# A new order table, its second gate ahead of a buffer's reuse, and column means of w1 in place of a centring matrix

## The chip, the cores and the metric

One core of a Trainium2 chip. The metric is the device time of one execution in microseconds (us), on one core. The kernel runs five engines, each with its own fixed order of instructions: PE (TensorE, matmuls), DVE (VectorE), ACT (ScalarE), POOL (GpSimd) and SP (SyncE), which issues most loads and stores. Executions of one kernel agree within about 1 per cent here; some are in a slower state, which is told by its time and mostly goes with a lower clock. Medians and ranges are over all runs; ratios, and what is called the mean of the fast runs, leave the slow ones out. "Ratio" is the mean time of one kernel's fast runs over that of the other's fast runs of the same rounds on the same chip, so it is not quite the ratio of the medians that are quoted. The figure in brackets is its 95% interval.

## The reference, cut to what matters

```python
# q, k, v, a_re, a_im: (4, 8, 768, 48) float32
scale = min(|a|, 0.999) / (|a| + 1e-6);  a = a * scale      # complex decay
for t in range(768):
    S = a[t] * S + k[t] (x) v[t]                            # 48 x 48 a head, complex
    y[t] = q[t] @ Re(S)
x = y as (4, 768, 384)
xn = (x - mean(x)) / sqrt(var(x) + 1e-6) * g_ln
out = x + relu(xn @ w_ch1) @ w_ch2                          # 384 -> 1536 -> 384
```

The kernel does the recurrence in chunks of 128 steps: logarithm and angle of the decay are summed by matmuls, k and q are scaled by the exponentials and by sine and cosine (`ke`, `qe`, `ks`, `qs`), transposed, and multiplied (`am`, `atm`, `y`). Two chunks are a pair, and there are 12 pairs. The subtraction of the mean and g_ln are folded into w_ch1 once, at the start. "First-layer matmuls" are those with `w1b`, "second-layer" those with `w2b`.

## The kernel before: the parts that matter

Every operation is named (`l.3.0` is l of pair 3), and one table fixes the order of all of them on all engines. The letter is the engine, the digit a PSUM bank.

```python
RINGS = {"are": 3, "aim": 3, "q": 3, "k": 3, "vf": 2, ...}        # buffers of each tile
GATES = {"gate.0": "k.0.1", "gate.1": "aim.1.0"}
PLAN = """
... aim.3.0:S tab.trig.0:A th.0.0:A decc.0:V2 ph.0.0:P3
th.0.1:A aim.4.0:S th.1.0:A ...                                   # load of aim, pair 4
...
cos.2.0:A cos.1.0:A pad.ks.1:G gate.1:G ksT.1:V7 ...              # gate.1, much later
... v.0:G pad.qs.1:G ... qe.1.0.0:G ... wl.1:G ...                # POOL's order behind it
"""
# Graph.run: a buffer is checked only through the "uses" that an operation declares
for kind, idx in op.uses:
    for n in touch.get((kind, idx - self.rings[kind]), ()):
        assert n in done, (op.name, n)

def T(name, i):
    return tiles[name][i % RINGS[name]]                           # aim of pair 4 is aim of pair 1

def gate(name, t):                                                # no uses declared
    g.add(name, lambda: nc.gpsimd.tensor_copy(out=probe, in_=t()[:, 0, 0:1]), needs=[GATES[name]])
gate("gate.0", lambda: T("k", 0)[:, 1])
gate("gate.1", lambda: T("aim", 1))
# wl.0 and wl.1: POOL issues the loads of w1b and w2b behind gate.0 and gate.1

# mean folded into w1: gc = (I - 1/384) * g_ln; for each of 3 x 3 blocks (128 rows, 512 columns)
# 3 matmuls ("wp") and one write-back ("wc"): 27 matmuls, 9 copies on DVE or ACT
nc.tensor.matmul(bank(o), lhsT=gc[:, dc, ts(ec, C)], rhs=w1b[:, dc, ts(jb, 512)], ...)

# l: two DVE instructions
nc.vector.scalar_tensor_tensor(out=l, in0=r2, scalar=0.5, in1=w, op0=ALU.mult, op1=ALU.add)
nc.vector.tensor_scalar(out=l, in0=l, scalar1=LNCAP, scalar2=LNEPS, op0=ALU.min, op1=ALU.add)
```

Of the kernel before, what the change touches and what calls it, by code (L numbers as in the profile page):

```python
# [9 lines left out]
FP32 = mybir.dt.float32  # L10
# [23 lines left out]
GATES = {"gate.0": "k.0.1", "gate.1": "aim.1.0"}  # L34
# [5 lines left out]
ue:G car0.1:G are.0.0:S pad.ks.0:G car0.0:G tab.log.0:A ln.0.0:A iv.0.0:A ident:G cmat.0:G are.0.1:S one:G  # L40
zdec:G aim.0.0:S r.0.0:V ln.0.1:A iv.0.1:A aim.0.1:S are.1.0:S are.2.0:S aim.1.0:S r.0.1:V r2.0.1:V r2.0.0:A
u.0.0:A k.0.0:S gln:S k.0.1:S q.0.1:S aim.2.0:S q.0.0:S u.0.1:A ln.1.0:A iv.1.0:A uth:V vf.0.0:S vf.0.1:S
l.0.0:V warm.0:P1 warm.1:P1 warm.2:P1 warm.3:P1 warm.4:P1 warm.5:P1 warm.6:P1 warm.7:P1 warm.8:P1 warm.9:P1
warm.10:P1 warm.11:P1 warm.12:P1 warm.13:P1 warm.14:P1 warm.15:P1 warm.16:P1 warm.17:P1 warm.18:P1
warm.19:P1 warm.20:P1 warm.21:P1 warm.22:P1 dec.0.0:P0 l.0.1:V pick:G ln.2.0:A iv.2.0:A dec.0.1:P1 en.0.1:A1
en.0.0:A0 r.1.0:V r2.1.0:V e.0.1:A1 u.1.0:A cmat.1:G k.1.1:S q.2.0:S q.1.0:S ke.0.1.0:V q.1.1:S are.3.0:S
gate.0:G are.4.0:S vf.1.1:S k.1.0:S vf.1.0:S q.2.1:S e.0.0:A0 warm.23:P3 warm.24:P3 warm.25:P3 warm.26:P3
warm.27:P3 warm.28:P3 warm.29:P3 warm.30:P3 warm.31:P3 warm.32:P3 warm.33:P3 warm.34:P3 warm.35:P3
warm.36:P3 warm.37:P3 warm.38:P3 warm.39:P3 warm.40:P3 warm.41:P3 warm.42:P3 warm.43:P3 warm.44:P3 dps.0:P2
l.1.0:V warm.45:P3 warm.46:P3 warm.47:P3 dec.1.0:P4 aim.3.0:S tab.trig.0:A th.0.0:A decc.0:V2 ph.0.0:P3  # L50
th.0.1:A aim.4.0:S th.1.0:A ph.0.1:P2 r.2.0:V r2.2.0:V ke.0.0.0:V car.0.0:A3 abs.0.0:A3 cos.0.0:A car.0.1:V2
qe.0.1.0:V warm.48:P1 warm.49:P1 warm.50:P1 ph.1.0:P6 k.2.0:S k.2.1:S sin.0.0:A3 qe.0.0.0:V q.3.1:S
qs.0.0.1:V ks.0.0.0:V sin.0.1:A2 th.2.0:A abs.0.1:A2 cos.0.1:A car.1.0:V6 ph.2.0:P0 wl.0:G pad.qs.0:G
qs.0.1.1:V qs.0.0.0:V ks.0.0.1:V qs.0.1.0:V ks.0.1.0:V ks.0.1.1:V warm.51:P2 qT.0:P3 qsT.0:V3 sin.1.0:A6
abs.1.0:A6 kT.0:P2 ksT.0:V2 qT.1:P6 kT.1:P7 abs.2.0:A0 sin.2.0:A0 am.0:P2 cmat.2:G wgc:V pad.ks.2:G mask:G
cos.2.0:A cos.1.0:A pad.ks.1:G gate.1:G ksT.1:V7 qsT.1:V6 tab.log.1:A e.1.0:A4 atm.0:V2 wp.1.1:P0 wp.1.2:P1
wp.1.0:P7 wc.1.1:V0 wp.2.2:P6 am.1:P2 v.0:G pad.qs.1:G wp.2.1:P0 wc.1.0:V7 atm.1:V2 en.1.0:A4 gm.0:P7
u.2.0:A y.0:P4 qe.1.0.0:G G.0:A7 qe.1.0.1:G wp.0.1:P5 wp.2.0:P2 wc.1.2:V1 wl.1:G y.1:P3 x.0:A4 ln.3.0:A
qs.1.0.0:V l.2.0:V wc.2.2:A6 x.1:A3 wc.2.0:A2 xtr.0:P1 wp.0.2:P4 wp.0.0:P6 qs.1.0.1:V wc.0.1:V5 wc.2.1:A0
gm.1:P7 G.1:V7 wc.0.2:A4 aim.5.0:S q.3.0:S dec.2.0:P2 wc.0.0:A6 bn.1:V xtr.1:P0 xT.1:A0 xT.0:V1 e.2.0:A2  # L60
ke.1.0.1:G ke.1.0.0:G ks.1.0.1:V ks.1.0.0:V en.2.0:A2 iv.3.0:A ln.4.0:A v.1:A qT.3:P5 qT.2:P4 dps.1:P7
vf.2.1:S vf.2.0:S qe.2.0.1:G mm1.0.1.1:P0 mm1.0.1.0:P0 kT.3:P6 pad.qs.2:G qsT.3:V5 qsT.2:V4 kT.2:P2
mm1.0.0.1:P4 mm1.0.0.0:P4 relu.0.1:V0 ksT.2:V2 bn.0:V mm1.0.2.0:P0 k.3.0:S am.2:P2 qe.2.0.0:G ksT.3:A6
relu.0.0:A4 decc.1:A7 r.3.0:G gm.2:P6 qs.2.0.0:V mm1.0.2.1:P0 am.3:P4 iv.4.0:A G.2:A6 r2.3.0:A qs.2.0.1:V
qT.5:P7 gm.3:P6 atm.2:V2 atm.3:V4 y.2:P2 mm2.1.0:P3 y.3:P4 mm2.0.0:P5 mm2.1.1:P3 relu.0.2:V0 u.3.0:A r.4.0:G
rstd.0:G l.3.0:V x.2:A2 xtr.2:P2 mm2.0.1:P5 mm2.1.2:P3 x.3:V4 mm2.0.2:P5 k.4.0:S dec.3.0:P0 xtr.3:P4 k.3.1:S
ke.2.0.1:V r2.4.0:A u.4.0:A tab.trig.1:A th.3.0:A G.3:V6 qsT.5:V7 xT.2:A2 ot.1:V3 xT.3:V4 are.6.0:S
ke.2.0.0:G ks.2.0.1:G tab.log.2:A en.3.0:A0 ph.3.0:P6 e.3.0:A0 ot.0:V5 l.4.0:V ks.2.0.0:G mm1.1.0.0:P2
mm1.1.0.1:P2 dps.3:P4 qT.4:P5 mm1.1.1.1:P0 relu.1.0:V2 mm1.1.1.0:P0 mm2.2.0:P2 qsT.4:V5 decc.3:V4
tab.trig.2:A th.4.0:A mm1.1.2.1:P4 sin.3.0:A6 kT.4:P3 mm1.1.2.0:P4 bn.3:V abs.3.0:A6 qe.3.0.0:V qe.3.0.1:V  # L70
qs.3.0.1:V relu.1.1:A0 ksT.4:V3 cos.3.0:A v.2:G ke.3.0.1:G dec.4.0:P0 car.3.0:V6 relu.1.2:A4 mm2.3.0:P3
mm2.3.1:P3 mm2.3.2:P3 am.4:P6 gm.4:P4 mm2.2.1:P2 are.5.0:S ksT.5:S aim.6.0:S bn.2:V tab.log.3:A e.4.0:A0
en.4.0:A0 am.5:P0 G.4:A4 ke.3.0.0:G ks.3.0.1:V qs.3.0.0:V atm.4:V6 qT.6:P5 ks.3.0.0:G y.4:P4 kT.6:P6 kT.7:P7
atm.5:V0 y.5:P0 mm2.2.2:P2 ke.4.0.0:G ln.5.0:A rstd.1:G iv.5.0:A r.5.0:G ln.6.0:A x.4:A4 st.0:S x.5:A0
ksT.6:V6 st.1:S vf.4.0:S qsT.6:V5 dps.4:P6 xtr.5:P1 xtr.4:P0 am.6:P4 vf.3.0:S vf.3.1:S ksT.7:V7 decc.4:V6
iv.6.0:A tab.trig.3:A th.5.0:A r.6.0:G ph.4.0:P6 abs.4.0:A6 sin.4.0:A6 r2.6.0:A q.4.0:S xT.5:V1 xT.4:V0
mm1.2.2.0:P0 mm1.2.2.1:P0 q.4.1:S qe.4.0.0:G k.4.1:S vf.4.1:S car.4.0:A6 bn.4:V atm.6:V4 ot.2:V2 ot.3:V3
mm1.2.0.1:P4 mm1.2.0.0:P4 bn.5:V mm1.2.1.0:P2 v.3:G gm.6:P6 mm1.2.1.1:P2 qe.4.0.1:G y.6:P7 v.4:G relu.2.2:V0
relu.2.0:V4 x.6:V7 G.6:A6 ph.5.0:P0 relu.2.1:A2 ke.4.0.1:G qsT.7:S am.7:P4 k.5.1:S atm.7:V4 qs.4.0.1:G
mm2.4.0:P7 gm.7:P6 mm2.5.0:P2 r2.5.0:V are.7.0:S vf.5.0:S q.5.1:S th.6.0:A mm2.4.1:P7 sin.5.0:A0 cos.4.0:A  # L80
ks.4.0.0:V qs.4.0.0:V xtr.6:P3 y.7:P4 ks.4.0.1:V mm2.5.1:P2 mm2.5.2:P2 mm2.4.2:P7 x.7:V4 xtr.7:P5 qT.8:P4
rstd.2:G G.7:V6 xT.6:V3 tab.log.4:A u.5.0:A l.5.0:V abs.5.0:A0 u.6.0:A vf.5.1:S gm.8:P6 st.2:S q.5.0:S
oa.5:A2 v.5:G ot.5:G xT.7:A5 ln.7.0:A qsT.8:V4 are.8.0:S dec.5.0:P0 ot.4:V7 en.5.0:A0 e.5.0:A0 mm1.3.0.0:P2
mm1.3.0.1:P2 mm1.3.1.1:P4 mm1.3.1.0:P4 relu.3.0:A2 l.6.0:V qe.5.0.1:V G.8:V6 k.5.0:S relu.3.1:V4 ksT.8:S
ksT.9:S dec.6.0:P0 mm1.3.2.0:P2 mm1.3.2.1:P2 ln.8.0:A gm.9:P6 am.8:P4 mm2.6.0:P7 iv.7.0:A en.6.0:A0
ke.5.0.0:G ke.5.0.1:G aim.7.0:S qe.5.0.0:G qsT.9:S st.4:S q.6.1:S q.6.0:S k.6.0:S k.7.0:S e.6.0:A0 r.7.0:G
bn.7:V relu.3.2:V2 ph.6.0:P0 am.9:P2 atm.8:V4 mm2.7.0:P4 y.8:P5 iv.8.0:A tab.trig.4:A sin.6.0:A0 th.7.0:A
mm2.6.1:P7 qs.5.0.1:V r2.7.0:G qe.6.0.0:G atm.9:V2 y.9:P2 mm2.6.2:P7 mm2.7.1:P4 aim.8.0:S st.3:S vf.6.0:S
car.6.0:A0 x.8:A5 bn.6:V rstd.3:G x.9:V2 G.9:V6 bn.9:V ks.5.0.1:V abs.6.0:A0 cos.5.0:A qs.5.0.0:V cos.6.0:A
mm2.7.2:P4 xtr.9:P5 xtr.8:P6 ph.7.0:P2 oa.7:A4 ks.5.0.0:V qe.6.0.1:G ke.6.0.0:G xT.8:A6 dps.6:P4 xT.9:V5  # L90
r.8.0:G vf.6.1:S k.6.1:S ot.6:V7 car.7.0:A2 decc.6:V4 qT.10:P0 kT.10:P1 kT.11:P6 gm.10:P7 mm1.4.0.0:P4
mm1.4.0.1:P4 qsT.10:V0 abs.7.0:A2 qsT.11:S bn.8:V sin.7.0:A2 ksT.10:A1 am.10:P2 mm1.4.1.1:P0 ksT.11:V6
are.9.0:S vf.7.0:S st.5:S q.7.0:S G.10:V7 mm1.4.1.0:P0 am.11:P6 cos.7.0:A th.8.0:A tab.log.5:A u.7.0:A
relu.4.0:V4 ke.6.0.1:G qs.6.0.1:G relu.4.1:A0 v.6:G r2.8.0:A atm.10:V2 atm.11:V6 l.7.0:V qs.6.0.0:V
ks.6.0.1:V ks.6.0.0:V are.10.0:S mm1.4.2.1:P4 mm1.4.2.0:P4 ph.8.0:P2 y.11:P6 x.11:A6 y.10:P7 x.10:A7
ln.9.0:A dec.7.0:P0 q.7.1:S e.7.0:A0 en.7.0:A0 aim.9.0:S st.6:S iv.9.0:A rstd.4:G u.8.0:A qe.7.0.0:G ot.7:G
k.7.1:S vf.7.1:S mm2.8.0:P6 mm2.9.0:P7 mm2.8.1:P6 relu.4.2:V4 xtr.10:P4 xtr.11:P5 mm2.8.2:P6 xT.11:V5
xT.10:V4 mm2.9.1:P7 mm2.9.2:P7 bn.10:V r.9.0:V r2.9.0:V oa.8:A6 abs.8.0:A2 mm1.5.0.0:P0 mm1.5.1.1:P4
mm1.5.0.1:P0 kT.12:P6 mm1.5.1.0:P4 l.8.0:V ksT.12:V6 tab.trig.5:A sin.8.0:A2 relu.5.1:V4 mm1.5.2.0:P2
gm.12:P6 mm1.5.2.1:P2 k.8.0:S qsT.12:S qsT.13:S q.8.1:S am.12:P4 th.9.0:A ot.9:V7 relu.5.0:A0 ke.7.0.1:G  # L100
G.12:A6 qe.7.0.1:G qs.7.0.0:V qs.7.0.1:V ksT.13:S ph.9.0:P0 atm.12:V4 relu.5.2:A2 ke.7.0.0:G ks.7.0.1:V
ks.7.0.0:G gm.13:P6 am.13:P2 mm2.11.0:P7 vf.8.1:S q.8.0:S mm2.10.0:P4 mm2.10.1:P4 qT.14:P5 cos.8.0:A
sin.9.0:A0 car.9.0:V0 vf.8.0:S are.11.0:S k.8.1:S abs.9.0:A0 atm.13:V2 cos.9.0:A v.8:G y.12:P0 dec.8.0:P2
v.7:G y.13:P1 mm2.10.2:P4 G.13:V6 qsT.14:V5 bn.11:V k.9.0:S st.7:S gm.14:P6 dps.7:P5 tab.log.6:A en.8.0:A2
e.8.0:A2 u.9.0:A rstd.5:G ot.8:G aim.10.0:S x.12:V0 x.13:V1 xtr.13:P0 xtr.12:P1 ksT.14:S ksT.15:S qsT.15:S
# [93 lines left out]
def kernel(  # L199
# [12 lines left out]
    nc = tc.nc  # L212
# [559 lines left out]
```

## Time and profile before

| | before |
|---|---|
| time, median of 4 (range) | 209.06 us (207.92 to 211.78) |
| span of the profiled run | 206.8 us |
| first first-layer matmul | 46.67 us |
| last second-layer matmul ends | 203.31 us |
| PE, DVE, ACT, POOL busy | 176.3, 168.0, 156.9, 106.7 us |

In the groups by line and shape, a row gives line, engine, operation, tile written and read, count, then busy us, mean ns of one, and the idle time in front:

```profile
L455 DVE SCALAR_TENSOR_TENSOR l<-r,w 128x768 f16<-128x768 f16 x11 | 13.7, 1241 | 1.0 <-ACT r L451 1.0
L457 DVE TENSOR_SCALAR l<-l 128x768 f16<-128x768 f16 x11 | 7.7, 704 | 0.4
```

These are l's two steps: 1241 and 704 ns in the mean, while undisturbed ones take 951 and 360. The rest I read as time in which DVE stands behind POOL at the port they share.

### The profile page before, as it was taken

The numbers are of one execution on the slowest core, as the hardware profiler recorded it, in microseconds if no ns is written. First come the engines' busy times: TensorE is split into PE (matmuls) and PEld (weight loads), VectorE is DVE, ScalarE is ACT, GpSimd is POOL, SyncE is SP. The second block draws the span as 40 slices with busy tenths as digits, with TensorE's granted clock in tenths as the row PEclk, the third lists the DMA queues.
The fourth block names the chain that finished last, engine by engine and source line by source line (L and its number), as shares of the span: only waits on it lengthen the run. The fifth ranks groups of instructions, "written<-read, shape, count | busy, mean of one in ns | idle before, by whom it ended". The sixth has DMA issues, their size and how long they took to land.

```text
span 206.8 us, 5060 instructions
## 1 busy us (share of the span) xinstructions
PE 176.3 (85%) x1999; PEld 132.6 (64%) x2001; DVE 168.0 (81%) x276; ACT 156.9 (76%) x219; POOL 106.7 (52%) x131
## 2 busy tenths in 40 slices
PE   5666930689998899989979997997999899999993
PEld 4444710367766588677658674786687677977771
DVE  0679960299999899999999899799998997774752
ACT  5799960389999999999979894898799958743210
POOL 8472000858756579649794491355457813514330
PEclk9999995599999999999999997899999999999998
DMA  5999999999808995979989999999999989695322
GB/s 141 281 223 205 176 267 250 225 163 193 207 4 118 257 199 122 240 128 249 217 157 259 230 178 190 241 174 230 176 225 230 174 100 235 170 203 109 116 76 76
DMA packets 135271, 38.34 MB, mean 185 GB/s; under 512 B 130256, under 2 KB 134864, under 8 KB 135248
## 3 DMA queue, kind: packets, MB, share of 16 engines
q1 hardware_dynamic: 133296, 35.66, 83.6%
q0 software_dynamic: 1952, 2.36, 6.8%
q8 instruction: 15, 0.25, 0.5%
q14 instruction: 8, 0.07, 0.2%
HBM read 28.31 MB, written 4.72 MB: 160 GB/s over the span
## 4 chain that ended last, share of the span: by engine, by line
PE 42%; DVE 31%; issue 18%; POOL 7%; ACT 1%; POOLq 0%; DVEq 0%
PE banks L706 14%; PE banks L685 13%; DVE l L455 5%; DVE atm L277 4%; PE banks L590 4%; DVE ks L277 3%; DVE h L698 3%; PE banks L483 2%; DVE qs L277 2%; DVE stats L653 2%; PE banks L465 2%; PE banks L640 2%; DVE x L274 1%; PE banks L567 1%; DVE ot L720 1%
## 5 line engine op out<-in xcount | busy, mean ns | idle before, releaser
L706 PE MATMUL banks<-w2b,h 128*128 128x384 bf16 x288 | 54.1, 327 | 2.6 <-DVE G L277 1.2
L685 PE MATMUL banks<-xT,w1b 128*128 128x256 bf16 x432 | 52.5, 272 | 0.1
L685 PEld LDWEIGHTS <-w1b 128*128 128x128 bf16 x432 | 41.1, 98 | 6.5 <-DVE xT L274 0.3
L706 PEld LDWEIGHTS <-h 128*128 128x128 bf16 x288 | 26.5, 98 | 17.1 <-issue 2.8
L277 DVE TENSOR_TENSOR atm<-banks,mask 128x1024 bf16<-128x1024 f32 x24 | 28.9, 1215 | 4.7 <-PE banks L590 4.2
L696 ACT ACTIVATE h<-banks 128x1024 bf16<-128x1024 f32 x20 | 20.4, 1022 | 11.1 <-PE banks L685 11.0
L277 DVE TENSOR_TENSOR qs<-qe,trig 128x768 bf16<-128x768 bf16 (+1 forms) x23 | 13.5, 606 | 11.4 <-POOL qe L277 11.1
L277 POOL TENSOR_TENSOR qe<-q,e 128x384 bf16<-128x384 f32 x16 | 17.4, 1090 | 8.8 <-ACT e L469 5.9
L698 DVE TENSOR_SCALAR h<-banks 128x1024 bf16<-128x1024 f32 x16 | 19.3, 1212 | 2.8 <-PE banks L685 2.8
L740 ACT ACT_TABLE_LOAD x16 | 20.5, 1283 | 1.1 <-PEq L756 0.8
L277 POOL TENSOR_TENSOR ke<-k,en 128x384 bf16<-128x384 f32 x16 | 16.5, 1042 | 5.6 <-ACT en L469 2.9
L277 POOL TENSOR_TENSOR r<-aim,are 128x768 f16<-128x768 f32 x8 | 14.9, 1859 | 8.2 <-ACT are L439 7.6
L618 PE MATMUL banks<-v,ks 128*128 128x48 bf16 x160 | 7.5, 186 | 12.2 <-POOL v L403 10.4
L618 PEld LDWEIGHTS <-ks 128*128 128x128 bf16 x160 | 7.0, 99 | 14.4 <-issue 10.8
L455 DVE SCALAR_TENSOR_TENSOR l<-r,w 128x768 f16<-128x768 f16 (+1 forms) x13 | 14.7, 1135 | 1.0 <-ACT r L451 1.0
L590 PE MATMUL banks<-qsT,ksT 128*128 128x128 bf16 x192 | 15.0, 223 | 0.3 <-DVE h L698 0.2
L272 ACT CAST G<-banks 128x384 bf16<-128x384 f32 x9 | 4.3, 478 | 14.0 <-PE banks L618 13.9
L403 POOL TENSOR_SCALAR v<-vf 128x768 bf16<-128x768 f32 x11 | 10.3, 942 | 8.0 <-PE banks L483 4.6
L277 DVE TENSOR_TENSOR ks<-ke,trig 128x768 bf16<-128x768 bf16 (+1 forms) x21 | 13.8, 680 | 0.2
L590 PEld LDWEIGHTS <-ksT 128*128 128x128 bf16 x192 | 12.4, 99 | 1.9 <-issue 0.5
L718 POOL TENSOR_TENSOR ot<-ot,x 128x384 f32<-128x384 f32 x9 | 8.3, 931 | 9.7 <-ACT ot L711 9.7
L653 DVE BATCH_NORM_STATS2 stats<-x 128x6 f32<-128x384 bf16 x24 | 13.1, 548 | 0.1
(90 smaller groups left out, 395.8 us busy)
## 6 DMA issues: line engine op xcount, KB each, us to landing
k<-in_k_dram SPq DMA_DIRECT2D x24, 192.0 KB, 4.4
q<-in_q_dram SPq DMA_DIRECT2D x24, 192.0 KB, 3.7
vf<-in_v_dram SPq DMA_DIRECT2D x24, 192.0 KB, 4.1
out_dram<-ot SPq DMA_DIRECT2D x24, 192.0 KB, 2.8
are<-in_a_re_dram SPq DMA_DIRECT2D x11, 384.0 KB, 4.6
aim<-in_a_im_dram SPq DMA_DIRECT2D x11, 384.0 KB, 4.7
w1b<-in_moe_w_ch_dram POOLq DMA_DIRECT2D x1, 1152.0 KB, 10.5
w2b<-in_moe_w_ch_dram POOLq DMA_DIRECT2D x1, 1152.0 KB, 12.5
```

The source lines that it names most:

```text
L277: {"DVE": nc.vector, "POOL": nc.gpsimd}[eng(name)].tensor_tensor(**kw)
L403: {"DVE": nc.vector, "POOL": nc.gpsimd}[eng(nm)].tensor_scalar(out=T("v", P), in0=T("vf", P), scalar1=1.0, scalar2=0.0, op0=ALU.mult, op1= ...
L455: nc.vector.scalar_tensor_tensor(out=S_("l"), in0=S_("r2"), scalar=0.5, in1=S_("w"), op0=ALU.mult, op1=ALU.add)
L590: nc.tensor.matmul(ps[:, h], lhsT=T("ksT", n)[:, h], rhs=T("qsT", n)[:, h], start=True, stop=True)
L618: nc.tensor.matmul(heads(ps)[:, h], lhsT=T("ks", P)[:, c, h], rhs=T("v", P)[:, c, h], start=nfirst, stop=True, skip_group_check=True)
L653: nc.vector.bn_stats(out=T("stats", n), in_=T("x", n))
L685: nc.tensor.matmul(ps[:, jj], lhsT=w1b[:, dc, ts(gi * JG + jj, C)], rhs=T("xT", P)[:, dc].rearrange("p c t -> p (c t)"), start=(dc == 0), ...
L696: act(out=dst, in_=src, func=AF.Relu)
L698: nc.vector.tensor_scalar(out=dst, in0=src, scalar1=0.0, scalar2=None, op0=ALU.max)
L706: nc.tensor.matmul(bank(f"o.{n}")[:, 0:DM], lhsT=T("h", P)[:, j, ts(c, C)], rhs=w2b[:, j], start=(j == 0), stop=(j == NJ - 1))
L718: nc.gpsimd.tensor_tensor(out=T("ot", n), in0=T("ot", n), in1=T("x", n), op=ALU.add)
L740: g.add(f"tab.{nm}.{i}", lambda tab=tab: nc.scalar.preload_act_table_set(tab))
```

## The change

Its intent: a new order table found by a search that models the shared port ("taken in turns"), so that DVE and POOL should hinder each other less; a gate that declares which buffer it reads; and fewer matmuls for the folded mean, since g_ln * (w - column mean) needs only the column means. The transposition xT may also go by DMA, and does so for 2 of 24. The table also moves work between engines (relu from DVE to ACT, ks from DVE to POOL). It is 100 lines, and is cut here.

```diff
-GATES = {"gate.0": "k.0.1", "gate.1": "aim.1.0"}
+GATES = (("k", 0, 1), ("aim", 1, 0))
 PLAN = """
-... aim.4.0:S ... wl.0:G ... gate.1:G ... v.0:G ... qe.1.0.0:G ... wl.1:G ...
+... r2.0.0:G gate.1:G q.0.0:S ... gate.0:G ... wl.0:G ... wl.1:G ... aim.4.0:S ...
-    def gate(name, t):
-        g.add(name, lambda: nc.gpsimd.tensor_copy(out=probe, in_=t()[:, 0, 0:1]), needs=[GATES[name]])
+    for i, (nm, P, c) in enumerate(GATES):
+        g.add(f"gate.{i}", lambda nm=nm, P=P, c=c: nc.gpsimd.tensor_copy(
+            out=probe, in_=(T(nm, P)[:, c] if nm in "kq" else T(nm, P))[:, 0, 0:1]),
+            needs=[f"{nm}.{P}.{c}"], uses=[(nm, P)])
-    for dc in range(ND):
-        g.add(f"cmat.{dc}", lambda dc=dc: c_cmat(dc))
+    g.add("cmean", lambda: nc.gpsimd.memset(cmean, 1.0 / DM))
     for jb in range(NG):
+        o = f"wp.{jb}"
+        def wp(jb=jb, o=o):
+            for dc in range(ND):
+                nc.tensor.matmul(bank(o), lhsT=gc[:, dc], rhs=w1b[:, dc, ts(jb, 512)],
+                                 start=(dc == 0), stop=(dc == ND - 1))
         ...
         for ec in range(ND):
-            (a wp of three matmuls, and a copy to w1b on DVE or ACT)
+            g.add(f"wc.{jb}.{ec}", lambda jb=jb, ec=ec, o=o: nc.vector.scalar_tensor_tensor(
+                out=w1b[:, ec, ts(jb, 512)], in0=w1b[:, ec, ts(jb, 512)], scalar=gln[:, ds(ec, 1)],
+                in1=bank(o), op0=ALU.mult, op1=ALU.subtract), needs=[o], ps=(o, 1))
 ...
+            (xT.n: by DMA where the table gives it to SP)
```

## The prediction

> **What bounds the kernel now.** I began with the busy table and the 40 slices, because the program runs in fixed order on five engines and the first question is whether one engine is full or all of them wait.
>
> ```profile
> PE 176.3 (85%) x1999; PEld 132.6 (64%) x2001; DVE 168.0 (81%) x276; ACT 156.9 (76%) x219; POOL 106.7 (52%) x131
> ...
> PE   5666930689998899989979997997999899999993
> ...
> DVE  0679960299999899999999899799998997774752
> ACT  5799960389999999999979894898799958743210
> POOL 8472000858756579649794491355457813514330
> PEclk9999995599999999999999997899999999999998
> DMA  5999999999808995979989999999999989695322
> ```
>
> A slice is 206.8 / 40 = 5.17 us. Three engines are near 80%, so the table names no single bound; the slices do better. In slice 6 (31.0 to 36.2 us) PE, DVE, ACT and POOL all show 0, and the PE clock is halved in slices 6 and 7. From slice 8 DVE and PE are close to full, ACT a little less. So there are three regimes: a start, a hole, and a dense part.
>
> The list of waits says what the hole is, and the order of time says when:
>
> ```profile
> POOL probe L351 <- DMA aim<-in_a_im_dram: 20.1, 1, 20.1
> ...
> DVE qs L277 <- POOL qe L277: 11.1, 1, 11.1
> ...
> PE banks L618 <- POOL v L403: 10.4, 1, 10.4
> ```
>
> ```profile
> 28.45 0.68 DVE L274 CAST w1b<-banks 128x512 bf16<-128x512 f32 x1
> ...
> 36.89 0.70 SPq L434 DMA_DIRECT2D aim<-in_a_im_dram  x1
> 37.01 0.18 POOL L351 COPY probe<-aim 128x1 f32<-128x1 f32 x1 [20.11 <-DMA aim<-in_a_im_dram]
> 37.16 0.83 POOL L403 TENSOR_SCALAR v<-vf 128x768 bf16<-128x768 f32 x1
> ...
> 38.04 0.48 PE L618 MATMUL banks<-v,ks 128*128 128x48 bf16 x8 [10.38 <-POOL v L403]
> ```
>
> One POOL instruction of 183 ns, the gate that holds back the load of the second weight, waits 20.1 us. Behind it in POOL's order stand v of pair 0 and qe of pair 1; PE waits 10.4 us for the one and DVE 11.1 us for the other. Between 29.13 (DVE's last end) and 37.01 no engine computes: 7.9 us.
>
> Why so long? The gate is meant to read aim of pair 1, the seventh load. aim has three buffers, pair 4 uses pair 1's, and in the order table before, aim.4.0 stands ahead of gate.1. The gate declares no use of the buffer, so nothing objected, and it waits for pair 4's load, the 27th of the sync queue: issued about 32, landed 37.0. The compiled order agrees: the gate waits on lane 2 of eight, and 27 is lane 2 counting from 0, while the seventh would be lane 6.
>
> Then what limits the dense part? The first-layer matmuls start at 46.67, so it lasts 160 us. The chain of waits is on DVE until about 67, mixed until 147, and from there on PE; it gives PE's true pace, which the busy time does not:
>
> ```profile
> 199.40 3.91 PE banks L706 x24
> ...
> 195.47 3.93 PE banks L685 x36
> ```
>
> That is 0.163 us for a second-layer matmul and 0.109 for a first-layer one. With 288 and 432 of these, 192 of the score products at 0.45/8, 512 small ones of 48 columns at about 0.026, and some 30 us of transposes, phases, decays and the rest, PE needs about 140 us of the 160. There are some 15 to 20 us of bubbles to win at most, plus the ends.
>
> **What the Trainium skill says.**
> 1. "SBUF — State Buffer", Who interferes with whom: a DVE instruction with two SBUF inputs contends with a GpSimd one that reads SBUF, and a DVE instruction in a 2-port mode with any GpSimd one; the later one blocks for the whole instruction. The trace agrees that DVE instructions are stretched: the large l takes 951 ns in the median of the tile view (all shapes) against a mean of 1241, its second step 360 against 704, ks 548 against 757, with single ones up to 2157.
> 2. "TensorE: Matmul & The Clock Gate", What's actually happening: an idle window of about 3.4 us halves the array's clock. The trace agrees: clock 0.50 from 32 to 40 us, and six 512-column matmuls took 2.73 us right after the hole, five 1.24 us later.
> 3. "ScalarE: Activation LUTs", What ACT_TABLE_LOAD costs: 1283 ns plus a drain of about 1380. The trace has 16 loads at a mean of 1283, but the next activation starts 0.01 us after one (13.87 + 1.28, then 15.16), so I count 1.28 only.
>
> **The change part by part.**
>
> *Gate.* It now declares its use of the buffer, and in the new table stands before aim.4.0; the compiled order shows it waiting on lane 6, the seventh load. The 7.9 us hole goes, with about 1 us of ramp (v, then qe on POOL before DVE restarts at 40.24) and about 1 us of half-clock matmuls. Against that, while nobody computed the loads ran ahead at about 260 GB/s; that lead is lost.
>
> *The new start, walked by hand along ACT,* which stands idle only about 3.6 us in the first 28. From 3.44 (the first load landed), ACT's instructions up to the second xT of pair 0, with durations from the groups by shape, sum to 6.5 (logs, exponentials, first decays) + 6.2 (table, angles, sines) + 4.9 + 4.7 + 10.2 = 32.5, of which four tables are 5.1. That is 35.9 us, about 37.5 with small waits. The first weight load is issued later than before: after ks of pair 0 and the mask on POOL, I get about 19.5 instead of 11.9; with the 10.5 us it took to land, 30, just before its first use. First layer one can thus start near 38 to 39 instead of 46.7. About **8 us** come from here.
>
> *Column means.* Instead of subtracting the mean through 27 matmuls with a centring matrix, 3 groups of 3 give the column means. 18 fewer, at 0.22 to 0.25 us in pace, is 4 us of PE, but most of it lay at 23.7 to 27.5 in the shadow of the hole and 38.7 to 43.5 after it; I count it inside the 8. The write-back was 4 on DVE at 676 and 5 on ACT at 592 ns (5.7 us); now it is 9 on DVE. The similar ot instruction of 384 columns takes 608 ns, so 512 may take about 740: 6.7 us on DVE, 4.0 more, at a place where DVE is not yet full. ACT loses 3.0. POOL loses the centring matrix, 3 x (0.42 + 0.79) = 3.6.
>
> *Moves in the dense part,* counts from the two tables times the row means. DVE: relu 16 to 9 (-8.5), ks 21 to 15 (-4.5), r2, qs, ke, r, x, car and decc (about -7), abs +5 (about +4.5), ot +5 (+3.0), v +3 (+2), ksT and xT (+1.7), write-back +4: about -5. ACT: relu +7 (+7.2), tables 16 to 20 (+5.1), abs -5 (-4.0), oa -5 (-2.9), write-back -3, rest +5: about +7, to some 164. POOL: ks +6 (+11), qs +2, r and r2 +1 each, v and ot -5 each (-9.4), centring -3.6: about +5. PE: 31 more warm-up matmuls that fill idle time, 3 more transposes.
>
> *Port in turns.* Means less medians over the large DVE instructions (l 0.29 x 11 + 0.34 x 11, ks 0.21 x 17, qs 0.11 x 19, ke 0.23 x 8, qe 0.09 x 8, r2 0.24 x 5) make about 16 us of the 168. A table whose search knew of these waits should lose fewer, and above all should not hand PE a late operand because of one. I put this at 4 us of the end, an estimate: a third of the stretch, or a quarter of PE's 15 to 20 us of bubbles.
>
> Sum: 209.6 - 8 - 4 - 1 (last stores, pieces) = **196.5 us**.
>
> **The rivals.**
> 1. *The start only.* The dense part is bound by PE at 140 us plus dependences, and ACT gets 7 us more with four more tables. Then only the 8 us remain: 201 to 202. For it: the tail from 147 is all PE. Against it: PE has visible bubbles at 104 to 108, 124 to 128 and 140 to 144 (2.5 to 2.8 us busy of 4).
> 2. *The lost lead returns as load waits.* DMA is busy in nearly every slice to 175 us[...]. For it: a shorter kernel moves the same 38.3 MB. Against it: after the start, waits on loads are some 6 us in all, and busy shares over 1.0 show that this column counts overlaps. Cost 3 to 6 us: 200 to 203.
> 3. *POOL becomes the late one.* It takes 6 more ks at 1.8 us each, against 0.55 to 0.76 on DVE. If PE or the transposes wait on them, 2 to 5 us are lost: 199 to 202.
> 4. *The search pays in full.* The stretch on DVE halves and PE runs almost without bubbles: 38.5 + 140 + 8 of bubbles + 4 for the end: 190 to 191.
>
> **Range and chances.** The hole's cause is certain and its removal worth about 4%, so within 2% (over 205.4) needs two rivals together or a new accident in the order. Range 190.5 to 203, faster 0.94, within 2% 0.05, slower 0.01.
>
> **What would show it.** Right: the gate on aim waits no more than a few us, no slice with all engines at 0, no half clock near 35, first-layer matmuls from about 38, DVE busy about 155 to 163, ACT about 164, means of l, its second step and ks nearer 951, 360 and 548. Wrong: a new wait over 5 us on POOL's ks or on a load; first-layer matmuls after 43; a dense part still 160 us long, which would make the search worth nothing; or one of 150 or less, which would make it worth more than I say.

## The result, and the profile after

| | before | after |
|---|---|---|
| time, median of 4 (range) | 209.06 (207.92 to 211.78) | 198.25 (197.11 to 198.66) |
| ratio | | 0.9491 [0.9423, 0.956] |
| span of the profiled run | 206.8 | 196.2 |
| first first-layer matmul | 46.67 | 39.68 |
| last second-layer matmul ends | 203.31 | 192.55 |

Correct, and 10.8 us faster by the medians. The page's busy row and slices (one is now 196.2 / 40 = 4.9 us):

```profile
PE 178.8 (91%) x2031; PEld 135.7 (69%) x2032; DVE 160.1 (82%) x268; ACT 164.1 (84%) x226; POOL 107.8 (55%) x127
...
PE   4987566999999999999999997999999999998992
...
DVE  1449999899999999999998799799969969935702
ACT  4799994989899999999999999897979998565160
POOL 8535558515839359135968699315891376530230
PEclk9999965599999999999999999999999999999999
DMA  5999999999899399899799999999998999994222
```

No slice has all engines at 0 any more, and PE is at 9 nearly everywhere from slice 7 on. But the PE clock still falls in slices 5 to 7. POOL's instructions in order of time (start, duration, engine, line, what, and in brackets the wait and what ended it) show the gates at work:

```profile
9.07 0.18 POOL L347 COPY probe<-aim 128x1 f32<-128x1 f32 x1 [0.63 <-DMA aim<-in_a_im_dram]
...
17.80 1.01 POOL L350 DMA_DIRECT2D w1b<-in_moe_w_ch_dram  x1
```

The gate on aim waits 0.63 us instead of 20.11. The end of the chain is the same two groups at the same pace as before:

```profile
184.71 3.93 PE banks L684 x36
188.64 3.91 PE banks L705 x24
```

So the 10.8 us come from two places: 7.0 us before the first first-layer matmul (46.67 to 39.68), and 3.8 us between it and the end (156.6 to 152.9 us). The sums of busy time from 40 us on, of before and then of after, show the second:

```profile
sum 168.00, PE 154.44 PEld 117.49 DVE 147.34 ACT 130.02 POOL 92.29; mean PE 7.35 PEld 5.59 DVE 7.02 ACT 6.19 POOL 4.39
```

```profile
sum 168.00, PE 148.94 PEld 114.82 DVE 130.94 ACT 131.98 POOL 83.93; mean PE 7.09 PEld 5.47 DVE 6.24 ACT 6.28 POOL 4.00
```

From 40 us to its last end PE is idle 163.3 - 154.4 = 8.9 us before and 152.6 - 148.9 = 3.6 us after.

The port, in the groups by shape of after:

```profile
L449 DVE SCALAR_TENSOR_TENSOR l<-r,w 128x768 f16<-128x768 f16 x11 | 11.5, 1044 | 0.3 <-ACT r L445 0.3
L451 DVE TENSOR_SCALAR l<-l 128x768 f16<-128x768 f16 x11 | 10.6, 968 | 0.4
L371 DVE SCALAR_TENSOR_TENSOR w1b<-w1b,gln,banks 128x512 bf16<-128x512 bf16 x9 | 6.1, 736 | 0.9 <-PE banks L367 0.9
```

l's first step came down (1241 to 1044 ns), its second went up (704 to 968). Instruction by instruction the reason can be seen, first DVE, then POOL:

```profile
21.98 1.86 DVE L451 TENSOR_SCALAR l<-l 128x768 f16<-128x768 f16 x1
...
31.25 1.85 DVE L451 TENSOR_SCALAR l<-l 128x768 f16<-128x768 f16 x1
```

```profile
21.78 1.84 POOL L280 TENSOR_TENSOR r<-aim,are 128x768 f16<-128x768 f32 x1 [2.98 <-ACT are L433]
...
30.36 2.52 POOL L280 TENSOR_TENSOR r<-aim,are 128x768 f16<-128x768 f32 x1 [0.50 <-ACT are L433]
```

POOL's r ends at 23.62 and 32.88, and DVE's step, 0.36 us of work, ends 0.22 us later both times (23.84, 33.10). Where no POOL instruction runs (68.36, 102.09, 130.08 us) it takes 0.36. In the second case POOL's own r, 1.81 us otherwise, took 2.52: DVE's first step was there ahead of it. Each waits for the whole instruction of the other.

### The profile page after: what moved, and what is told of

It is laid out like the page before. It is cut to its first block, busy times and chain, and to the rows that moved or that the text cites. A ratio compares the mean times of both kernels' runs of the same rounds, so it can differ in the third digit from the quotient of the medians.

```text
span 196.2 us, 5114 instructions
## 1 busy us (share of the span) xinstructions
PE 178.8 (91%) x2031; PEld 135.7 (69%) x2032; DVE 160.1 (82%) x268; ACT 164.1 (84%) x226; POOL 107.8 (55%) x127
## 4 chain that ended last, share of the span: by engine, by line
PE 50%; DVE 20%; ACT 10%; DMA 8%; SPq 5%; issue 4%; POOL 2%; DVEq 0%; POOLq 0%
PE banks L705 16%; PE banks L684 15%; DVE atm L280 5%; DMA are<-in_a_re_dram 4%; SPq L566 3%; PE banks L584 3%; DVE l L449 3%; PE banks L459 3%; DVE h L697 2%; DVE l L451 2%; PE banks L561 2%; DMA q<-in_q_dram 2%; DMA out_dram<-ot 2%; ACT L739 2%; PE banks L655 2%
## 5 line engine op out<-in xcount | busy, mean ns | idle before, releaser
L695 ACT ACTIVATE h<-banks 128x1024 bf16<-128x1024 f32 x27 | 27.0, 1022 | 5.2 <-PE banks L684 5.0
L739 ACT ACT_TABLE_LOAD x20 | 25.7, 1283 | 1.1 <-PEq L755 0.8
L280 POOL TENSOR_TENSOR ks<-ke,trig 128x768 bf16<-128x768 bf16 (+1 forms) x11 | 17.9, 1634 | 12.0 <-DVE ke L280 7.4
L280 POOL TENSOR_TENSOR r<-aim,are 128x768 f16<-128x768 f32 (+1 forms) x9 | 16.5, 1836 | 11.0 <-ACT are L433 11.0
L719 DVE SCALAR_TENSOR_TENSOR ot<-banks,rstd,x 128x384 f32<-128x384 f32 x20 | 12.0, 610 | 8.7 <-PE banks L705 6.0
L584 PE MATMUL banks<-qsT,ksT 128*128 128x128 bf16 x192 | 15.3, 227 | 1.2 <-DVE qsT L277 1.2
L734 PE MATMUL banks<-u_e 128*128 128x256 f16 x83 | 12.5, 318 | 2.8 <-POOL u_e L312 2.8
L634 PE MATMUL banks<-v,atm 128*128 128x48 bf16 x192 | 12.2, 186 | 1.5 <-DVE atm L280 1.4
L449 DVE SCALAR_TENSOR_TENSOR l<-r,w 128x768 f16<-128x768 f16 (+1 forms) x13 | 12.9, 990 | 0.9 <-ACT r L445 0.8
L634 PEld LDWEIGHTS <-atm 128*128 128x128 bf16 x192 | 10.8, 97 | 3.7 <-DVE atm L280 2.8
L734 PEld LDWEIGHTS <-u_e 128*128 128x128 f16 x83 | 9.4, 113 | 5.0 <-POOL u_e L312 2.4
L477 PE MATMUL banks<-th,u_th 128*128 128x384 f16 (+1 forms) x52 | 12.1, 320 | 0.7 <-ACT th L467 0.7
## 6 DMA issues: line engine op xcount, KB each, us to landing
w1b<-in_moe_w_ch_dram POOLq DMA_DIRECT2D x1, 1152.0 KB, 10.1
```

The source lines that it names most:

```text
L280: {"DVE": nc.vector, "POOL": nc.gpsimd}[eng(name)].tensor_tensor(**kw)
L449: nc.vector.scalar_tensor_tensor(out=S_("l"), in0=S_("r2"), scalar=0.5, in1=S_("w"), op0=ALU.mult, op1=ALU.add)
L477: nc.tensor.matmul(heads(ps[:, c]), lhsT=u_th[:, c, j], rhs=step(T("th", P), j), start=False, stop=(j == R - 1))
L584: nc.tensor.matmul(ps[:, h], lhsT=T("ksT", n)[:, h], rhs=T("qsT", n)[:, h], start=True, stop=True)
L634: nc.tensor.matmul(ps[:, h], lhsT=T("atm", n)[:, h], rhs=T("v", P)[:, c, h], start=True, stop=nfirst)
L695: act(out=dst, in_=src, func=AF.Relu)
```

## The experiments

All twelve (e1 to e3 with the changed kernel again; e7 to e10; e11, e12, e5 and e6). Each is compared with runs of the kernel before on the same chip (medians 209.49 to 210.63 us). All results are correct unless said otherwise. They fall in four questions.

| run | what it is | median us | ratio to before |
|---|---|---|---|
| after_again | the changed kernel again | 198.15 | 0.9446 [0.9384, 0.9508] |
| e1_gate | before + gate moved | 208.31 | 0.9929 [0.9857, 1.0001] |
| e2_gate_means | e1 + column means | 205.43 | 0.9749 [0.9658, 0.9841] |
| e3_means_27 | after with 27 mean matmuls | 197.42 | 0.9423 [0.9366, 0.948] |
| e7_before_smallw | before, little weight loaded | 204.17 | 0.9773 [0.9667, 0.9879] |
| e8_gate_smallw | e1, little weight loaded | 198.13 | 0.9428 [0.9345, 0.9512] |
| e9_after_smallw | after, little weight loaded | 199.83 | 0.9534 [0.9472, 0.9597] |
| e10_gate_w2late | e1, w2 load later | 208.08 | 0.9902 [0.9799, 1.0005] |
| e11_gate_pair4_late | e1, pair 4's loads later | 207.28 | 0.9882 [0.9785, 0.9979] |
| e12_after_w1_early | after, w1 load earlier | 198.7 | 0.9477 [0.9418, 0.9537] |
| e5_l_early | after, l ahead of POOL's r | 199.27 | 0.9521 [0.9443, 0.9599] |
| e6_both | e5 + PE kept busy | 200.52 | 0.9546 [0.9465, 0.9627] |

### What is the gate worth by itself?

**The gate alone.** The table of before, with one word moved:

```diff
-... th.0.1:A aim.4.0:S th.1.0:A ... pad.ks.1:G gate.1:G ksT.1:V7 ...
+... th.0.1:A gate.1:G aim.4.0:S th.1.0:A ... pad.ks.1:G ksT.1:V7 ...
```

> The kernel before with one entry of its order table moved: the gate on aim of pair 1 now stands ahead of the load of pair 4 that reuses the buffer. My theory: the stretch of 7.9 us in which no engine computes is gone with its ramp, the first-layer matmuls start near 38 to 39 us instead of 46.7, the span ends 7 to 9 us sooner (time near 200.5 to 202, ratio to before 0.96), and the half clock near 35 us is gone. Rival (the lead that the loads won in the hole was needed): the first-layer matmuls start early but waits on loads come back, and the time falls by 4 us or less (205 or more).

A miss: 208.31 us, 0.7 per cent, not clear of noise. The hole did go: the first first-layer matmul starts at 36.0 us, 10.7 us ahead of before. But l of pairs 2, 3, 4 and 5 starts at 30.9, 51.5, 58.4 and 88.7 us against 41.5, 56.1, 61.2 and 88.7: the lead is 10.6, then 4.6, 2.8 and 0. From 72 us on PE and DVE follow before's profile at nearly the same clock times. The waits (engine, line, tile, what was waited for, us in total, times, longest):

```profile
POOL qe L274 <- DMA q<-in_q_dram: 8.5, 2, 8.3
```

and POOL, in order of time:

```profile
41.64 0.92 POOL L274 TENSOR_TENSOR qe<-q,e 128x384 bf16<-128x384 f32 x1 [8.33 <-DMA q<-in_q_dram]
...
43.85 3.88 POOL L274 TENSOR_TENSOR r<-aim,are 128x768 f16<-128x768 f32 x2
```

One wait on a load has taken the place of another. q of pair 2 was issued at about 31 us and landed at 41.6; w2 (issued at 29.5) and the aim of pairs 3 and 4 (issued from 31.0 on) were under way beside it. The chain of this run goes through the aim of pair 4 (issued at 33.6, landed at 44.3), so q was not the only late load. Then POOL's backlog held the port for 3.9 us, a qs on DVE took 4.2 us, and PE stood still for 6.0 us (its clock from 40 to 72 us was 0.84 in the mean, against 0.97 before). The GB/s row of the page shows why, for before, for this run and for after:

```profile
GB/s 141 281 223 205 176 267 250 225 163 193 207 4 118 257 199 122 240 128 249 217 157 259 230 178 190 241 174 230 176 225 230 174 100 235 170 203 109 116 76 76
```

```profile
GB/s 145 273 219 199 179 265 175 211 217 250 196 144 188 178 134 62 241 163 224 231 109 267 214 164 210 253 184 250 218 153 236 156 115 205 192 214 105 116 76 76
```

```profile
GB/s 138 250 220 233 170 233 173 184 242 217 187 250 222 70 172 245 226 230 238 148 226 205 223 163 280 188 212 253 184 222 155 156 203 147 238 197 130 104 84 82
```

Summed from the left with the length of a slice, before has moved 7.98, 9.98 and 12.05 MB by 36.2, 46.5 and 56.9 us; the gate alone 7.53, 9.75 and 12.06 MB by 36.2, 46.6 and 57.0. The transfers arrive at the same clock times with or without the hole. At its first first-layer matmul, before had some 10 MB in hand and this run 7.5. The hole was the time in which the loads ran ahead. The kernel after rides nearly the same curve (7.85 MB by 39.2, 10.1 by 49.0, 12.25 by 58.9 us).

**With little weight to load.** If the loads are what takes the lead back, taking bytes away must give it back. Both weight loads are cut to a twelfth, and the rest of both weights is filled with a constant; the result is wrong.

```diff
-    out=w1b, in_=moe_w_ch1.rearrange("(dc p) j -> p dc j", p=C)), needs=["gate.0"])
+    out=w1b[:, 0, 0:DM], in_=moe_w_ch1.rearrange("(dc p) j -> p dc j", p=C)[:, 0, 0:DM]), needs=["gate.0"])
-    out=w2b, in_=moe_w_ch2.rearrange("(jc p) e -> p jc e", p=C)), needs=["gate.1"])
+    out=w2b[:, 0], in_=moe_w_ch2.rearrange("(jc p) e -> p jc e", p=C)[:, 0]), needs=["gate.1"])
+    nc.vector.memset(w1b.rearrange("p d j -> p (d j)").bitcast(FP32), 0.00996)
+    nc.vector.memset(w2b.rearrange("p d j -> p (d j)").bitcast(FP32), 0.00996)
```

On the kernel before:

> The kernel before with the two weight loads cut to one part in twelve (the rest of the weights is filled with a constant in the first 5 us on DVE), so the result is wrong on purpose; everything else, the late gate too, is as it was. It takes 2.2 of the 8.8 MB out of the first 40 us. If the loads bound the start of the program, the gate's load (the 27th) lands some us earlier and the hole shrinks: first-layer matmuls 2 to 5 us before 46.7, time 204 to 208. If the gate alone is the cause and loads are not, the time stays at 208 to 210.

Measured 204.17 us; the gate, still in its old place, waits 15.3 us instead of 20.1. On the gate alone:

> The kernel with the gate alone moved, and the same two weight loads cut (wrong result on purpose). New theory, after the gate alone gave only 0.7%: its lead of 10 us is eaten because the second weight load now leaves at 29.5 us and shares the DMA engines with the loads of pair 2 and the angles, POOL waits 8.3 us for q, and its two r that follow back to back hold DVE's qs for 4.2 us. With the weight loads gone the wait for q is under 2 us and the time falls to 199 to 202. Rival (the dense part of the old order is bound by something else and would absorb any lead): 206 or more.

Measured 198.13 us (its profiled run, slow, shows no wait of an engine on a load over 0.5 us between 26 and 80 us). So with light loads the gate is worth 0.9428 / 0.9773 = 0.965, or 6.1 us between the means of the fast runs (203.8 and 197.7); with the full loads about 1.5. **The same edit is worth 6 to 7 us or 1.5 us by whether the loads behind it arrive.** On the kernel after:

> The changed kernel with the weight loads cut in the same way (wrong result on purpose). If the new table's gain is that it fits the work to the arrival of the loads, it has little to win from lighter loads: 195 to 198. If its start is as load bound as the old one's, 190 to 193.

199.83 us, outside both ranges: no gain. The two fills stand at the head of DVE's order, and l of pair 1 starts at 22.8 us instead of 21.0, so a gain of up to 1.8 us could be hidden; the 5 us and more of a start that hangs on the weight loads could not.

### Can the old order be mended by moving a load?

**w2 later**, behind POOL's qe of pair 2:

```diff
 PLAN (of e1): wl.1:G moved from behind qe.1.0.1:G to just ahead of r.3.0:G
```

> The kernel with the gate alone moved, right result, and the second weight load moved on POOL from before ke of pair 1 to after qe of pair 2, so that q of pair 2 lands first. New theory: the wait of 8.3 us for q falls to 4 us or less, and the time lies between the gate alone (208.3) and the gate with small weights, at 202 to 206. If the order of the loads is not what ate the lead, it stays at 207 to 209.

208.08 us, a miss. The wait for q is gone, and PE waits for w2 instead:

```profile
PE banks L703 <- DMA w2b<-in_moe_w_ch_dram: 6.4, 1, 6.4
```

**Pair 4 later.**

```diff
 PLAN (of e1): are.4.0:S aim.4.0:S moved to just ahead of q.3.1:S
```

> The kernel before with gate.1 ahead of aim.4.0 as in the first experiment, and the two loads of pair 4's half (are.4.0 and aim.4.0) moved behind k.2 in the sync queue, just before q.3.1. Theory 'the old load order cannot follow the earlier start': pair 2's k and q land about 3 us sooner than in the first experiment (there q.2.1 landed at 41.6 and POOL waited 8.3 us for it), POOL's two r of pairs 3 and 4 no longer stand back to back, DVE's qs is not held for 4.2 us, and the time comes to 203 to 206. Rival 'a load moved is a wait moved': another load, r.4's or w2's, is waited for instead, and the time stays at 207 to 209.

207.28 us: the theory misses, the rival holds. The wait for q is gone, and ACT waits for what was moved:

```profile
ACT w L434 <- DMA are<-in_a_re_dram: 9.4, 2, 8.1
```

Two loads moved, and each became the wait. These two moves do not mend the old order; that no move could is not shown.

**w1 earlier in the new order**, where before had it:

```diff
 PLAN (of after): wl.0:G moved to directly behind gate.0:G (issued at 13.3 us instead of 17.8)
```

> The changed kernel with the load of the first weight issued right behind gate.0, at about 12.8 us instead of 17.8, as the old table has it. Theory 'the new table is fitted to when loads arrive': 4.7 MB of weight then goes ahead of pair 1's inputs, k, q or vf of pair 0 or 1 are waited for 2 to 6 us, first-layer matmuls start at 40 to 43 instead of 39.6 and the time is 199.5 to 202. Rival 'the start has slack for loads': same within 0.5 per cent (197.5 to 199), or the first-layer matmuls come sooner.

198.7 us, first first-layer matmul at 39.5: the rival holds. v of pair 0 came later (PE waits 2.6 us for it, and POOL's r 8.0 us on ACT's v), but the end did not move. The new order has room for this load where the old one had none for the two that were moved. (The expectation's 4.7 MB is both weights; the page puts w1 at 1152 KB as written.)

### What are the column means worth?

**Column means in the old order**, with the gate moved: one wp for each block, nine write-backs on DVE, `cmean` in place of the three `cmat`.

```diff
 (definitions of cmean, gc, wgc, wp, wc as in the change, in the kernel of e1)
-cmat.0:G ... cmat.1:G ... cmat.2:G ... wp.1.1:P0 wp.1.2:P1 wp.1.0:P7 wc.1.1:V0 ... wc.2.2:A6 ...
+cmean:G ... wp.1:P0 wc.1.1:V0 wp.2:P6 ... wc.1.0:V0 ... wp.0:P5 ... wc.2.2:V6 ...
```

> The same with the column means of the change added, in the old order: 9 matmuls of 512 columns instead of 27, the write-back 9 times on DVE at about 0.74 us instead of 4 on DVE and 5 on ACT. My theory: within 1.5 us of the run with the gate alone, because the 18 matmuls saved are 4 us at full clock in a stretch where DVE and ACT are as full as PE, and DVE gets 4 us more. Rival (the means carry much of the gain): 3 us or more faster than the gate alone. What then still lies between this and the changed kernel is the new order table: I expect 2 to 4 us.

205.43 us, from 202.59 to 205.47 in the four fast runs; two runs were slow. By the means of the fast runs (204.4 and 208.3) this is 3.9 us better than the gate alone, and the intervals of the two ratios do not overlap: my theory (within 1.5 us) misses, and the size is the rival's. In the profiled run, the fastest of the six, POOL's two r are apart (43.2 and 47.0 us), and the long qs of e1 does not occur; how much of the 2 per cent is that, and how much the means, this run cannot tell.

**All 27 matmuls in the new order.** Each accumulation is done three times, with the same result:

```diff
+            for rep in range(3):
-            for dc in range(ND):
+                for dc in range(ND):
```

> The changed kernel with each accumulation of the column means done three times over in its bank (27 matmuls as before, same result). In its profile the PE clock is half from 25 to 38 us, and the 9 matmuls take 0.43 us each in pace. If they stand on the path there, 18 more cost up to 7.7 us; the second and third group follow the decay of pair 2 directly, so I expect the first-layer matmuls 3 to 6 us later (43 to 45.5) and the time 2 to 5 us longer. If the means do not matter, as I had counted, the time is within 1 us.

197.42 us against 198.15 for the changed kernel, intervals overlapping, and the first first-layer matmul at 40.3 us instead of 39.7: 18 more matmuls cost nothing. The row of these matmuls, after and then here:

```profile
L367 PE MATMUL banks<-w1b,gc 128*128 128x512 bf16 x8 | 4.2, 630 | 0.2 <-issue 0.2
```

```profile
L368 PE MATMUL banks<-w1b,gc 128*128 128x512 bf16 x27 | 8.0, 456 | 0.0
```

PE's clock came back sooner with them (0.76 instead of 0.50 from 32 to 36 us), so that one took 456 ns instead of 630. The run asks about PE's matmuls alone, not about the write-backs or about what POOL and ACT are spared. The changed kernel itself, again, for these comparisons:

> The changed kernel unaltered, on the same chip as the partial kernels: 198 us, ratio to before 0.943 to 0.956. It is here so that the parts can be compared in one set of rounds.

### Are the port's turns and the half clock what is left?

**l ahead of POOL's r.**

```diff
 PLAN (of after): u.1.0:A l.1.0:V moved ahead of ks.0.0.0:V;  l.2.0:V moved ahead of atm.0:V2
```

> The changed kernel with l.1.0 (and u.1.0) ahead of ks.0.0.0 and l.2.0 ahead of atm.0 in the table, so that l's second step of pairs 1 and 2 starts before POOL's r does. Theory 'whoever comes second to the port waits for the whole instruction': the second step of pairs 1 and 2 takes 0.36 us instead of 1.86, first-layer matmuls start 1 to 2 us sooner (38 to 38.8), and the time is 196 to 197.7. Rival 'the end is set elsewhere, or another DVE instruction pays instead': the two steps are short but ks, r2 or another takes what they give back, and the time stays within 0.4 per cent of 198.

The rival holds, in its second form. l's second step:

```profile
L447 DVE TENSOR_SCALAR l<-l 128x768 f16<-128x768 f16 x11 | 7.7, 696 | 0.4
```

696 ns instead of 968: both 1.86 us turns are gone from l, 3.0 us in all. But they were not removed. The half-width ks and qs that now follow l stand behind POOL's r in its place, after and then here:

```profile
L280 DVE TENSOR_TENSOR ks<-ke,trig 128x384 bf16<-128x384 bf16 x3 | 1.0, 356 | 0.3 <-ACT trig L502 0.3
L280 DVE TENSOR_TENSOR qs<-qe,trig 128x384 bf16<-128x384 bf16 x4 | 2.0, 510 | 0.1
```

```profile
L276 DVE TENSOR_TENSOR ks<-ke,trig 128x384 bf16<-128x384 bf16 x3 | 2.6, 892 | 0.3 <-ACT trig L498 0.3
L276 DVE TENSOR_TENSOR qs<-qe,trig 128x384 bf16<-128x384 bf16 x4 | 3.2, 824 | 0.1
```

They take 2.8 us more. So this run does not tell what a turn is worth. e12 comes nearer to that: there both second steps take 0.36 us as well (the row is the same, 696 ns), ks and qs are not longer than after (352 and 484 ns), and the time is 198.7 us; but it moved a load too. In e5 the first first-layer matmul starts at 38.8 us, 0.9 earlier. But l of pair 3 starts at 45.7 (45.8 after), the first-layer matmuls of pair 1 at 56.0 (56.1), and the time is 199.27 us, not better than 198.15.

**The same, with PE kept busy** by 46 more warm-up matmuls between 19 and 33 us:

> As the run before (l early), with 46 more warm-up matmuls in PE's gaps between 19 and 33 us. Theory 'PE's clock is halved there because PE is idle too much': the clock stays at 0.9 or more from 25 to 38 us, the matmuls of the weight's means take 0.3 to 0.4 us instead of 0.63, and 0 to 1.5 us are won beyond the run before (195.5 to 197.5). Rival 'PE is not on the path there': clock full, time the same within 0.3 per cent. The tripled means have shown the second already for matmuls that bring the clock back; this asks it for the whole stretch.

```profile
PEclk9999999999999999999999999999999999999999
```

The clock is full throughout, and the time is 200.52 us: no gain (means of the fast runs 200.2, and 199.0 for the run before). But this does not show that the half clock is free. In the profile of the run before, the clock was 0.57 from 24 to 28 us and full from 28 on, and its mean matmuls took 378 ns already, as they do here. The 46 matmuls also stand in the way: the first first-layer matmul comes at 39.7 us instead of 38.8. And of the fast runs of e5, the three with a mean clock of 0.98 or more took 198.0 to 198.5 us, the two with 0.966 took 200.1 and 200.2. Whether the half clock costs 0 or some 2 us stays open.

## Why the prediction was right, and where a step failed

The total (196.5 predicted, 198.25 measured) lies in the range, and its two main terms, the start and the dense part, were measured nearly as written. But the trace's division by time is not the same as a division by cause, and that is where a step fails; and each of the two terms was reached by a working that is partly wrong.

- **The hole's cause: right.** The gate waited for the load of a later pair in the same buffer; it waits 0.63 us now.
- **The new start along ACT: right in time, 1 us short, only in part right in the path.** The second xT was put at 35.9 to 37.5 and ended at 38.49; the first first-layer matmul at 38 to 39, and it came at 39.68. The term "8 us" measured 7.0. There is some luck in it: ACT worked 29.9 us from 3.44 to 38.49 (32.5 predicted) and stood idle for 5.2 (1.6 allowed). Between 28 and 40 us it was busy for 8.2 of 12; the chain runs there over DVE (both long second steps of l) and PE at half clock.
- **"Its removal worth about 4%", said of the hole: wrong as a cause.** Removing the hole alone gives 1.5 us in the old order (e1), because the load lead is lost with it. That is rival 2, which I priced at 3 to 6 us for the changed kernel (against it I said that waits on loads were some 6 us in all after the start; from 40 us on they add up to 9.5 in the trace). There it doesn't hold (the longest wait on q is 3.6 us, and taking the weights' bytes away gains nothing seen); for the gate alone it holds in full, at some 9 of 10.7 us. The whole change is worth 10.8 us; the gate alone 1.5. The rest needs an order that can use the time.
- **PE's need, "about 140 us of the 160": mis-summed.** The five terms in the prediction (46.9 + 47.1 + 10.8 + 13.3 + 30) add up to 148, and the 160 us run to the end of the span; from the first first-layer matmul to the last second-layer one it was 156.6. So there were some 8 us of bubbles to win, not 15 to 20. The trace agrees with the right sum: PE was busy 148.5 us of that stretch before, and 149.3 of 152.9 after.
- **The order, "4 us": right as the dense part's gain (3.8 us; PE's idle time from 40 us on 8.9 to 3.6), by luck: it was taken as a quarter of 15 to 20 us, and is about half of 8. It is far too small as what the table does.** From the gate alone to the whole change is 0.9929 to 0.9446, some 10 us, and from the gate with column means 0.9749 to 0.9446, some 6 us. What the table owes to its order and what to the work that it moves is not separated.
- **The port's turns as its means: not shown, and the sign of one was wrong.** I expected l's second step nearer 360 ns; it rose from 704 to 968. l's first step, ks (757 to 673) and ke (778 to 547) did come down, and with the counts of after the stretch over the large instructions fell from about 16.4 to 10.4 us. What that is worth no run shows: e5 only moved the two longest turns that remain.
- **Column means: right to count them inside the 8.** The write-backs took 736 ns each (740 estimated), and PE's 18 matmuls are worth nothing there (e3). In the old order the whole of it gave about 3.9 us (e2), for a reason that is not known.
- **Engine sums: right.** DVE 160.1 (155 to 163 said), ACT 164.1 (164). POOL rose by 1.1 us, not 5.
- **No half clock near 35: wrong.** The clock was 0.69, 0.50, 0.50 and 0.60 in the four stretches of 4 us from 24 to 40 us; at full clock the time was no better (e6), but its cost is not settled.
- **Rivals 1 and 3** did not occur: the dense part did get shorter; no wait on POOL's ks over 5 us arose. **Rival 4** came true in its bubbles (3.6 us, under the 8 that it allows) and failed in its 140 us for PE, which are 149.

What stays open: which property of the new table gives its room. It consumes nearly the same bytes at the same clock times, and is at l of pair 5 at 76.0 us instead of 88.7; that it asks for loads in the order in which they arrive is what e1, e10, e11, e8 and e12 suggest together, but no run changed that alone. The new table with the gate in the old place was not run either. A further rival stands untested: the table relieves DVE (168.0 to 160.1 us busy), which held the chain until 67 us before, and no run moved that work alone. No version beat the changed kernel beyond the spread.

## What to carry to other kernels

A hole in which all engines wait is also a time in which the loads run ahead: before counting it as gain, sum the bytes moved up to its end, and ask whether the work behind it would still find its inputs. If a removed wait gives nothing, follow the lead from stage to stage (here 10.7, 4.6, 2.8, 0 us) to the wait that took it back, and test it by taking bytes away rather than by moving a load, since a moved load can become the wait itself. And a helper that reads a tile only to hold something back must declare that use: this one waited 20 us for a buffer's next owner, and no check saw it.

## What the Trainium skill lacked or had wrong

- "SBUF — State Buffer", Who interferes with whom: its rule that the port is an exclusive lock agrees with every case looked at. For a DVE instruction behind POOL's it has no figure for the end of the wait (it has one only for POOL's DMA issue behind DVE): DVE's step of 0.36 us ended 0.22 us after POOL's instruction each time (1.86 and 1.85 us in all), and POOL is held likewise (2.52 us instead of 1.81).
- "TensorE: Matmul & The Clock Gate", What's actually happening: it ties the half clock to an idle window of about 3.4 us. In the changed kernel the clock was 1.00 to 25.5 us and 0.52 in the half us after that, although PE was recorded busy for 1.69 us of the 3.5 ahead, with no gap over 1.31 us. (In e5, with 0.28 us busy from 20 to 24, the clock was 0.57 from 24 to 28, as the page has it.) A later section, A second HAM failure mode, tells of frequent short idles that do the same. How much work inside a window counts as busy is not on the page.
- "ScalarE: Activation LUTs", What ACT_TABLE_LOAD costs: 1283 ns agrees (20 loads in the changed kernel, mean 1283). The drain of about 1380 ns is not seen: the next activation starts 0.01 us after the load's end (10.75 + 1.28, then 12.04).
- No page has the case of a gate that reads a rotating buffer after its next owner's load was put ahead of it: 20.1 us of wait, and no check that objected.
- No page says how to value a hole by what the loads do in it: the same edit gave 1.5 us with the weights loaded in full and 6 to 7 us with a twelfth of them.
